# A linear-attention block gated by an MLP mixer: Gram products of the first two tiles beside WQ's column means, and w1's column means from rounded parts

## Chip, cores and metric

The kernel runs on one core of one Trainium2 chip. The metric is device time in microseconds (us) of one execution; lower is better. The kernel before was timed three times. One more execution was taken with the hardware profiler; its records are called the trace, and its summary the page.

## What is computed

The inputs are x (2048 rows of 512), the attention weights wqkv and wo, and the mixer weights w1 to w4. The core of the reference is this:

```python
xn = _layernorm(x)
# s: linear attention, 32 heads of width 16
q, k, v = heads(xn @ wqkv)
phi = lambda t: jnp.where(t > 0, t + 1, jnp.exp(t)) + 1e-6
kv = einsum("bhsd,bhse->bhde", phi(k), v)
z = einsum("bhsd->bhd", phi(k))
num = einsum("bhqd,bhde->bhqe", phi(q), kv)
den = einsum("bhqd,bhd->bhq", phi(q), z)[..., None] + 1e-6
s = (num / den) @ wo
# B: spatial-shift mixer, then channel MLP, both on xn
h = gelu(_layernorm(xn) @ w1)
x1 = xn + shift(h) @ w2        # quarters of h shifted by +1, -1, +2, -2 rows
B = x1 + gelu(_layernorm(x1) @ w3) @ w4
return x + s * silu(B)
```

## The kernel before

The 2048 rows are 16 tiles of 128 rows (`NT`), in four blocks of four tiles (`QT`). Nearly every product on TensorE is made from rounded parts: an fp32 operand is split into a high part of the type fp32r, copied by ScalarE (`pl.act(hi, ..., AF.Copy)`), and a low part, the rest, subtracted by VectorE (`split`). `rounded` does both. `products` then makes three products, high by high, high by low and low by high. A few products are made in plain fp32 (`slow=True`). In the trace one of these has two records.

The layer normalization is folded into the products. x is multiplied raw (transposed, as `xt`), and its column means enter through the weights: `Weights.center` adds up the four 128-row chunks of a weight (tile `wqt` for WQ, `w1t` for w1), multiplies the sum by a matrix of ones (PSUM tile `wqm` or `w1m`, line 577) and subtracts the mean from the chunks (line 579). For WQ the sum is made by three VectorE additions; for w1, with `by_dma`, by one load and three accumulating DMAs on GpSimd's queue. The K weights are treated another way: their column sums (`wkt`, then `ksum`) become the tile `wneg`, and `feature_k` subtracts the mean of each row times that sum.

The first part of the program, up to about 80 us, is written in this order. WK and the transposed x of block 0 are loaded (`load_u(0, 2)`, in two pieces) and split. `load_rows` loads the first four row tiles, and ScalarE forms their sums (`sq`, with the helper columns `sx`) and squared sums. `raw_k` and `project` make the keys k0 to k3. `feature_k` turns them into features (tiles `kt`, `kr`, and the parts k0h, k0l and so on), and `halves_x` splits the normalized rows (x0h, x0l). Then WQ is centered and split, `gram(i)` adds the products of x and k of tile i to the four PSUM accumulators g (12 products a tile), and `query(i)` makes the queries (12 products a tile). Blocks 1 to 3 follow; w1 is centered in block 1 after key 6. The mixer's second product (`mix2`), the first MLP product (`up_pair`) and the product of queries and attention matrix (`attend_pair`) are made in Strassen form by the function `seven`: PSUM banks pb, pa and pe (with the suffix m in `mix2`, s in `attend_pair`) are filled in turns and read out by ScalarE or VectorE between two uses (tiles p1, p5, u2).

The order of instructions on each engine isn't the order in which the program is written. All operations are first recorded by `Plan.add`, each with an estimated cost; `deadlines` gives each a due time, worked backwards from the order of the TensorE operations; `nudged` makes some of them due earlier or later, by the table `SOONER` (pairs of operation number and steps of 0.25 us); and `emit` plays through the schedule and writes the instructions out one by one. A TensorE operation may go ahead of older ones within limits (`window` us of nominal TensorE time, `ahead` for those that take a new buffer), and a loading operation may start `lead` us before it is due. A changed table or limit can therefore move any instruction of any engine. What each engine issues is fixed at build time, and each engine's queue runs in order: an instruction that waits holds up all behind it.

The lines which the change touches are 565 to 579 (`Weights.center`), 1223 to 1234 (WQ, the Gram products and the queries), and 1413 to 1423 (the table and the limits). L146 in the profile is the line on which every matmul is issued, L167 every ScalarE operation, L189 to L199 the VectorE ones, L205 to L223 the DMAs.

Of the kernel before, what the change touches and what calls it, by code (L numbers as in the profile page):

```python
# [393 lines left out]
def linear_attn_gated_by_mixer(  # L394
# [43 lines left out]
    pl = Plan(nc, pools, counts, ("acc", "mm"))  # L438

    def piece(name, dt=F32):  # L440
        return pl.new("p", name, dt, PIECE)[:, :512]

    def rounds(name):

        return piece(name + "h", F32R), piece(name + "l", F32R)
# [4 lines left out]
    def bank(name):  # L450
        return pl.new("mm", name, F32, 512)[:, :]

    def fixed(name, n, dt=F32):

        t = pl.new("const", name, dt, n)
        t.ap = const.tile([P, n], dt, name=name)
        return t

    def both(pair, a, z):

        return tuple(v.cols(a, z) for v in pair)
# [5 lines left out]
    def split(out, full, hi):  # L467
        pl.tt(out, full, hi.f32, ALU.subtract)

    def products(ps, terms, start=True, stop=True, more=False, behind=None):  # L470

        ms = []
        for sh, sl, mh, ml in terms:
            ms += [(sh, mh), (sh, ml), (sl, mh)]
        for n, (s, m) in enumerate(ms):
            pl.mm(ps, s, m, start and n == 0, stop and n == len(ms) - 1, more=more, behind=None if n else behind)

    def rounded(hi, lo, full, src=None):

        pl.act(hi, src or full, AF.Copy)  # L480
        split(lo, full, hi)
# [9 lines left out]
    ident, ones, nhalf, zacc = fixed("ident", P), fixed("ones", P), fixed("nhalf", QT), fixed("zacc", 512)  # L491
    identr = fixed("identr", P, F32R)
    onesr, bmask, tiny, zmore = fixed("onesr", P, F32R), fixed("bmask", P), fixed("tiny", 1), fixed("zmore", 1)
# [45 lines left out]
    class Weights:  # L539
# [25 lines left out]
        def center(self, by_dma=False):  # L565

            t, r = piece(self.name + "t"), self.raw
            if by_dma:
                pl.load(t, self.src[:, 0])
                for c in range(1, NC):  # L570
                    pl.gather(t, self.src[:, c])
            else:
                pl.tt(t, r[0], r[1], ALU.add)
                pl.tt(t, t, r[2], ALU.add)
                pl.tt(t, t, r[3], ALU.add)
            ps = bank(self.name + "m")
            pl.mm(ps, ones.all, t, True, True, slow=True)
            for c in range(NC):
                pl.stt(r[c], ps, -1.0 / D, r[c], ALU.mult, ALU.add)

# [15 lines left out]
    def scale_x(lo, n):  # L596

        r = rs1[:, lo:lo + n]
        w = small(f"w{lo}", n).all
        pl.ts(w, var(mv1, lo, lo + n), EPS, None, ALU.add, eng="POOL")  # L600
        power(r, w, n)
        pl.ts(ns1[:, lo:lo + n], r, -1.0, None, ALU.mult, eng="POOL")
        pl.tt(nm1[:, lo:lo + n], means(mv1, lo, lo + n), ns1[:, lo:lo + n], ALU.mult, eng="POOL")
        for i in range(lo, lo + n):
            halves_x(i)
# [59 lines left out]
    def project(ps, i, ws, cs):  # L665
        b, j = divmod(i, QT)
        a = 2 + j * P
        products(ps, [ut(b, c, a, a + P) + ws.chunk(c) for c in cs], 0 in cs, NC - 1 in cs)
# [69 lines left out]
    def feature_k(i, ps):  # L738

        t, r = piece(f"kt{i}"), piece(f"kr{i}")  # L740
        pl.stt(t, wneg.all, mean(mv1, i), ps, ALU.mult, ALU.add)
        pl.act(r, t, AF.Relu, scale=col(rs1, i))
        pl.act(t, t, AF.Exp, scale=col(rs1, i))
        hi, lo = rounds(f"k{i}")
        pl.stt(r, t, 1.0, r, ALU.min, ALU.add)
        pl.act(hi, r, AF.Identity, bias=tiny.all)
        pl.stt(lo, r, TINY, hi.f32, ALU.add, ALU.subtract)
        pl.gather(zacc.all, r)
        GK[i] += (hi, lo)
# [14 lines left out]
    def query(i):  # L764
        ps = bank(f"q{i}")
        project(ps, i, WQ, range(NC))
        e, r = piece(f"qe{i}"), piece(f"qr{i}")
        pl.act(by_block(e), by_chunk(ps), AF.Relu, scale=col(ns1, i))
        pl.act(by_block(r), by_chunk(ps), AF.Relu, scale=col(rs1, i))
        pl.act(e, e, AF.Exp, scale=-1.0)  # L770
        pl.soon(pl.store(pqd[i].all, r))
        pl.soon(pl.gather(pqd[i].all, e))

    def gram(i):
        xh, xl, kh, kl = GK.pop(i)
        for c in range(NC):
            products(G[c].all, [both((xh, xl), c * P, (c + 1) * P) + (kh, kl)], i == 0, i == NT - 1)
# [442 lines left out]
    for i in range(2, QT):  # L1220
        project(ks[i], i, WK, range(1, NC))
        feature_k(i, ks[i])
    WQ = Weights("wq", wqkv[0])
    WQ.center()
    WQ.split()
    gram(0)
    query(0)
    query(1)
    load_u(1, 1)
    load_rows(QT)  # L1230
    scale_x(QT, 1)
    gram(1)
    query(2)
    gram(2)
    query(3)
# [69 lines left out]
    for base, s in ((0, 1), (DH - 1, -1)):  # L1305
        v = bmask.all.via(lambda ap: ap.rearrange("p (h d) -> p h d", d=DH))
# [16 lines left out]
    for gg in range(NC):  # L1323
        cs = gg * P, (gg + 1) * P
        ps = bank(f"kv{gg}").cols(0, P)
# [4 lines left out]
    for gg in range(NC):  # L1330
        ps = bank(f"m{gg}")
# [10 lines left out]
    for b in range(NQ):  # L1342
# [50 lines left out]
        else:  # L1393
# [3 lines left out]
            t = piece(f"xi{i}", F32R)  # L1397
# [13 lines left out]
                gate(b * QT + QT - 1, a, o, D // 2, late=True, by_dma=False, whole=o > 0)  # L1411

    SOONER = (
# [7 lines left out]
    )  # L1421
    pl.emit(first=6.0, lead={"p": 12.0, "w": 10.0, "ab": 10.0}, reserve={"p": 8, "w": 1, "ab": 0}, window=7.0,
            ahead=3.0, table=SOONER)


# [35 lines left out]
```

## Time and profile before

| | |
|---|---|
| time, median of 3 runs | 523.48 us (523.04 to 523.54) |
| time of the profiled execution | 523.29 us |
| its span, first to last instruction | 521.5 us |
| VectorE busy | 375.0 us (72%) |
| ScalarE busy | 328.7 us (63%) |
| GpSimd busy | 112.2 us (22%) |
| DMA | 100.11 MB, mean 192 GB/s |

The span starts with the program's first instruction; the profiled execution's time is 1.8 us longer than it. PE is TensorE's matmuls, PEld its weight loads, DVE is VectorE, ACT ScalarE, POOL GpSimd and SP SyncE. Rows of the timeline give start, length, engine, line, operation, written tile <- read tiles, and in brackets the idle time ahead and who ended it. Buffer numbers are left out of names: `k` can be k0 to k15, `w_s` a raw chunk of w1 or w2. The matmul records overlap, since matmuls are pipelined: the time that one takes from TensorE is read from start to start.

### The profile page before, as it was taken

The page shows a single profiled execution, that of the slowest core. Times are in us where ns is not written, and L with a number is a line of the kernel's source. Part 1 is how long each engine was busy: PE and PEld are TensorE (multiplying, and loading weights), DVE is VectorE, ACT ScalarE, POOL GpSimd, SP SyncE. Part 2 cuts the span into 40 slices and gives each one's busy share as a digit, 9 for nine tenths or more (in the row PEclk, how much of TensorE's full clock was granted, in tenths as well). Part 3 has the DMA queues.
Part 4 walks back from the last instruction along what each step waited for, and adds up shares of the span by engine and source line. Part 5 has one row for each costly group of instructions (what it writes and reads, how often), then busy time and mean ns, then how long its engine had stood idle before and what let it go on. Part 6 is the DMA issues. An engine that isn't in the chain of part 4 may idle for free.

```text
span 521.5 us, 8876 instructions
## 1 busy us (share of the span) xinstructions
PE 514.3 (99%) x3011; PEld 445.8 (85%) x3011; DVE 375.0 (72%) x748; ACT 328.7 (63%) x669; POOL 112.2 (22%) x207
## 2 busy tenths in 40 slices
PE   8999999999999999999999999999999999999996
PEld 5777788988888888898999889899898898999985
DVE  4974697559475837899998458886567867496635
ACT  5899784769558837769865656466463456544621
POOL 1777253140272022211100022000040000310000
PEclk9999999999999999999999999999999999999999
DMA  7959993375887189999685969848489466898704
GB/s 239 291 126 200 225 234 81 79 165 186 184 197 168 34 192 240 268 242 264 232 265 183 264 161 202 266 134 203 119 172 313 147 182 129 200 288 251 230 1 121
DMA packets 73856, 100.11 MB, mean 192 GB/s; under 512 B 7908, under 2 KB 31988, under 8 KB 73812
## 3 DMA queue, kind: packets, MB, share of 16 engines
q1 hardware_dynamic: 62724, 79.37, 49.5%
q0 software_dynamic: 11088, 20.19, 23.4%
q8 instruction: 23, 0.38, 0.3%
q14 instruction: 21, 0.17, 0.1%
HBM read 60.33 MB, written 30.81 MB: 175 GB/s over the span
## 4 chain that ended last, share of the span: by engine, by line
PE 93%; ACT 3%; DMA 2%; SPq 1%; DVE 1%; issue 1%; DVEq 0%; ACTq 0%
PE acc L146 23%; PE pb L146 11%; PE h L146 9%; PE g L146 8%; PE q L146 8%; PE pe L146 6%; PE k L146 5%; PE pbm L146 4%; PE pbs L146 3%; PE pa L146 3%; PE pem L146 2%; PE s L146 2%; PE a L146 2%; PE pes L146 2%; DMA wk_s<-in_wqkv 1%; PE pam L146 1%
## 5 line engine op out<-in xcount | busy, mean ns | idle before, releaser
L223 POOL DMA_DIRECT2D xo<-x1d x12 | 10.7, 1179 | 166.6 <-ACT xo L167 166.6
L223 POOL DMA_DIRECT2D th<-in_x x14 | 12.1, 868 | 72.2 <-DVE th L199 51.4
L167 ACT ACTIVATE p<-pb 128x256 f32<-128x256 f32 x20 | 7.7, 383 | 31.5 <-PE pb L146 31.4
L223 POOL DMA_DIRECT2D zacc<-kr x16 | 15.4, 963 | 52.4 <-DVE kr L199 43.5
L223 POOL DMA_DIRECT2D o<-x x16 | 14.6, 930 | 41.8 <-ACT o L167 19.9
L167 ACT ACTIVATE gf<-gf 128x256 f32<-128x256 f32 (+1 forms) x40 | 20.9, 523 | 0.9
L199 DVE SCALAR_TENSOR_TENSOR kt<-wneg,mv,k 128x512 f32<-128x512 f32 x16 | 11.8, 745 | 11.2 <-PE k L146 11.1
L167 ACT ACTIVATE ht<-ht 128x512 f32<-128x512 f32 x16 | 10.0, 630 | 15.5 <-DVE ht L189 15.5
L223 POOL DMA_DIRECT2D pqd<-qe x16 | 15.0, 938 | 19.6 <-DMA pqd<-qr 5.2
L199 DVE SCALAR_TENSOR_TENSOR kr<-kt,kr 128x512 f32<-128x512 f32 x16 | 11.1, 691 | 10.7 <-ACT kt L167 10.6
L167 ACT ACTIVATE th<-xo 128x512 f32<-128x512 f32 (+1 forms) x16 | 9.8, 616 | 13.4 <-DVE xo L189 11.7
L167 ACT ACTIVATE p<-pe 128x256 f32<-128x256 f32 x20 | 7.7, 384 | 12.3 <-PE pe L146 12.3
L189 DVE TENSOR_TENSOR gf<-pa,p 128x256 f32<-128x256 f32 x20 | 8.4, 422 | 9.3 <-ACT p L167 4.8
L189 DVE TENSOR_TENSOR ht<-h,abc 128x512 f32<-128x512 f32 x16 | 10.7, 687 | 5.8 <-PE h L146 5.3
L167 ACT ACTIVATE qe<-q,ns 128x512 f32<-128x512 f32 x16 | 10.9, 681 | 5.5 <-PE q L146 5.5
L167 ACT ACTIVATE x<-x,nm,rs 128x512 f32<-128x512 f32 x16 | 12.3, 807 | 3.2 <-POOL nm L189 3.2
L167 ACT ACTIVATE kr<-kt,rs 128x512 f32<-128x512 f32 x16 | 11.5, 717 | 3.6 <-DVE kt L199 3.5
L588 DVE BATCH_NORM_STATS2 st<-o 128x6 f32<-128x512 f32 x16 | 10.8, 686 | 3.2 <-DMA o<-x 3.2
L189 DVE TENSOR_TENSOR gf<-u,pe 128x256 f32<-128x256 f32 x20 | 8.3, 416 | 6.3 <-PE pe L146 6.3
L199 DVE SCALAR_TENSOR_TENSOR th<-th,so 128x512 f32<-128x512 f32 (+1 forms) x17 | 11.1, 658 | 2.3 <-ACT th L167 1.4
L167 ACT ACTIVATE y<-o,nm,rs 128x512 f32<-128x512 f32 x16 | 12.2, 802 | 0.0
L167 ACT ACTIVATE kt<-kt,rs 128x512 f32<-128x512 f32 x16 | 11.6, 724 | 0.4
(1567 smaller groups left out, 2195.0 us busy)
## 6 DMA issues: line engine op xcount, KB each, us to landing
w_s<-in_w SPq DMA_DIRECT2D x28, 256.0 KB, 4.4
x<-in_x SPq DMA_DIRECT2D x16, 256.0 KB, 5.1
zacc<-kr POOLq DMA_DIRECT2D x16, 256.0 KB, 5.3
pqd<-qr SPq DMA_DIRECT2D x16, 256.0 KB, 3.2
pqd<-qe POOLq DMA_DIRECT2D x16, 256.0 KB, 5.4
o<-x POOLq DMA_DIRECT2D x16, 256.0 KB, 4.8
x1d<-o SPq DMA_DIRECT2D x16, 256.0 KB, 4.0
pq<-pqd SPq DMA_DIRECT2D x16, 256.0 KB, 4.4
```

The lines of the kernel that those rows point to most:

```text
L146: lambda: nc.tensor.matmul(out.get(), lhs.get(), rhs.get(), start=start, stop=stop, skip_group_check=more))
L167: nc.scalar.activation(out.get(), src.get(), func, scale=get(scale), **kw)
L189: self.vec(eng, out, [a, b], lambda: self.e(eng).tensor_tensor(out.get(), a.get(), b.get(), op=op), True)
L199: lambda: self.nc.vector.scalar_tensor_tensor(out.get(), a.get(), get(s), b.get(), op0=op0, op1=op1),
L223: lambda: self.nc.gpsimd.dma_start(out.get(), get(src), accum_op=ALU.add), mb=mb)
L588: pl.add("DVE", .62, .69, [xv], [st], lambda: nc.vector.bn_stats(st.get(), xv.get()))
```

## The change

There are three edits. In `center`, when the sum came by DMA (which is w1 alone), the sum is split into rounded parts first, and two fp32r products with `onesr` (ones in fp32r) take the place of one fp32 product. `gram(0)` is written ahead of `WQ.center()`, and `gram(1)` directly behind `WQ.split()` instead of behind `scale_x(QT, 1)`. The planner's table is replaced, and its limits: lead of the tags p and w from 12 and 10 to 10 and 20, window from 7 to 9, ahead from 3 to 6.

```diff
@@ -574,7 +574,13 @@
             ps = bank(self.name + "m")
-            pl.mm(ps, ones.all, t, True, True, slow=True)
+            if by_dma:
+                ts = rounds(self.name + "m")
+                rounded(*ts, t)
+                for n, v in enumerate(ts):
+                    pl.mm(ps, onesr.all, v, n == 0, n == 1)
+            else:
+                pl.mm(ps, ones.all, t, True, True, slow=True)
             for c in range(NC):
                 pl.stt(r[c], ps, -1.0 / D, r[c], ALU.mult, ALU.add)
@@ -1221,15 +1227,15 @@
     WQ = Weights("wq", wqkv[0])
+    gram(0)
     WQ.center()
     WQ.split()
-    gram(0)
+    gram(1)
     query(0)
     query(1)
     load_u(1, 1)
     load_rows(QT)
     scale_x(QT, 1)
-    gram(1)
     query(2)
     gram(2)
@@ -1411,16 +1417,15 @@
     SOONER = (
-        15, 3112, 16, 652, 20, 3160, 24, 308, 25, 137, 27, 308, 28, 136, 31, 160, 33, 309, 34, 277, 36, 43,
+        15, 4865, 16, 1223, 20, 4844, 24, 462, 25, 213, 27, 466, 28, 198, 31, 318, 33, 493, 34, 350, 36, 61,
...
     )
-    pl.emit(first=6.0, lead={"p": 12.0, "w": 10.0, "ab": 10.0}, reserve={"p": 8, "w": 1, "ab": 0}, window=7.0,
-            ahead=3.0, table=SOONER)
+    pl.emit(first=6.0, lead={"p": 10.0, "w": 20.0, "ab": 10.0}, reserve={"p": 8, "w": 1, "ab": 0}, window=9.0,
+            ahead=6.0, table=SOONER)
```

In the order that the planner writes out, these instructions move:

- TensorE: `wqm` stays where it was, directly behind the last key product and ahead of the Gram products of tile 0. The 12 Gram products of tile 1 move from between and behind the products of queries 0 and 1 to behind the first six products of query 0. `w1m` stays behind key 6, as two products. After that the order is the old one but for some dozens of products near the edges of `seven` blocks, which change places with products around them.
- SyncE's queue: at the start the pieces of WK go one place ahead of the pieces of `xt`, and the load of x0 moves from between wk_s2 and wk_s3 to behind xt0_3. The load of x7 moves ahead of those of block 1's `xt`, and that of x4 between them; the fourth query store goes ahead of w1's loads. Loads and stores from 60 us on change places by one or a few.
- ScalarE: the first row sums of tile 0 move behind wk_3h and u_3h; x1, k1h, x1h and the two squared sums of tiles 2 and 3 move ahead of wq_2h; u_0h of block 1 and the normalizations of x5 to x7 move back; the new rounding of `w1t` stands behind the second `ar` copy and ahead of kr5.
- VectorE: kr1, k1l and x1l move ahead of WQ's chunks 2 and 3; the new subtraction of `w1t` stands behind k4l and ahead of kt5.
- GpSimd's queue: some halo pieces change places with the first accumulating DMA of `zacc` and with those of `w1t`; the fourth query's DMA moves ahead of block 1's halo.

11 rows, old and new, of the table SOONER are left out of this document.

## Prediction

> **What bounds the kernel now.** I read the page first, then TensorE's waits, then the start-to-start times of its products at the places that the change touches.
>
> ```profile
> span 521.5 us, 8876 instructions
> PE 514.3 (99%) x3011; PEld 445.8 (85%) x3011; DVE 375.0 (72%) x748; ACT 328.7 (63%) x669; POOL 112.2 (22%) x207
> PEclk9999999999999999999999999999999999999999
> ```
> ```profile
> PE k L146 <- ACT u_3h L167: 0.4, 1, 0.4
> PE wqm L146 <- DVE wqt L189: 0.3, 1, 0.3
> PE k L146 <- DVE wk_1l L189: 0.2, 1, 0.2
> PE k L146 <- DVE wk_2l L189: 0.2, 1, 0.2
> PE k L146 <- ACT wk_2h L167: 0.2, 1, 0.2
> ```
>
> The reader is to see that TensorE sets the time: it is busy for 99% of the span at full clock, and its only idle stretches behind the warm-up are these five, 1.3 us in all, every one before the first Gram product. So the change can gain in two ways alone, by less work on TensorE or by less waiting, and most of the waiting lies in the first 20 us. It can lose in any place where a producer comes late for TensorE.
>
> **w1's column means.** The first three rows are the old product and its neighbours, the last three the nearest relatives of the new one: products with `onesr` of a sum in rounded parts, made for z.
>
> ```profile
> 60.53 1.02 PE L146 MATMUL w1m<-w1t,ones 128*128 128x512 f32 x2
> 60.98 0.80 PE L146 MATMUL q<-wq_0h,u_0h 128*128 128x512 f32 x1
> 61.62 0.40 PE L146 MATMUL q<-wq_0l,u_0h 128*128 128x512 f32 x1
> ...
> 221.07 0.39 PE L146 MATMUL zp<-zsh,onesr 128*128 128x512 f32 x1
> 221.30 0.40 PE L146 MATMUL zp<-zsl,onesr 128*128 128x512 f32 x1
> 221.53 0.29 PE L146 MATMUL pbm<-w_b11h,ha113h 128*128 128x256 f32 x1
> ```
>
> From 60.53 to 61.62 TensorE makes the fp32 product and one fp32r product of 512 columns: 1.09 us. An fp32r product takes 0.23 us (221.07 to 221.30). After the change that stretch holds three of them, 0.69 us. The gain is 1.09 - 0.69 = 0.40 us, and it is on the path, since TensorE doesn't idle there. [...]
>
> The new work, one ScalarE rounding and one VectorE subtraction of 128x512, must be hidden. In the new order the rounding stands behind the second `ar` copy and the subtraction behind k4l:
>
> ```profile
> L223 POOL DMA_DIRECT2D w1t<-in_w x3: 895/912/1224, 22.7 to 39.3; - x3
> DMA to landing us min/median/max: 5.0/5.7/5.8
> ```
> ```profile
> 51.40 0.62 ACT L167 ACTIVATE qe<-qe 128x512 f32<-128x512 f32 x1
> 53.16 0.72 ACT L167 ACTIVATE kr<-kt,rs 128x512 f32<-128x512 f32 x1 [1.14 <-DVE kt L199]
> ```
> ```profile
> 51.53 0.69 DVE L199 SCALAR_TENSOR_TENSOR k4l<-kr,k4h 128x512 fp32r<-128x512 f32 x1 [1.28 <-ACT k4h L167]
> 52.38 0.75 DVE L199 SCALAR_TENSOR_TENSOR kt<-wneg,mv,k 128x512 f32<-128x512 f32 x1 [0.16 <-PE k L146]
> ```
>
> The third accumulating DMA is issued at 39.3 and lands by 45.1, some 6 us before the rounding's turn. ScalarE then idles 1.14 us and VectorE 1.28 us, so 0.62 and 0.69 us fit; kt5, queued behind the subtraction, may start some 0.5 us later. w1m is due at 60.5, 8 us on. I cost this at nothing. If the cover were gone, all of tile 5's features would come 0.5 us later, and with them a Gram product several microseconds away.
>
> **The start.** The wqm product isn't moved: the planner takes what is ready, and in the new order the Gram products of tile 0 still come behind it. So the 0.3 us at wqm goes only if wqt comes sooner. These rows show what it hangs on:
>
> ```profile
> 12.93 0.62 ACT L167 ACTIVATE sq<-x 128x512 f32<-128x512 f32 x1
> ...
> 14.60 0.72 ACT L167 ACTIVATE sq<-x,sx 128x512 f32<-128x512 f32 x1 [0.66 <-DVE sx L194]
> ...
> 15.66 0.60 ACT L167 ACTIVATE wneg<-ksum 128x512 f32<-128x512 f32 x1
> ```
> ```profile
> 13.73 0.70 DVE L189 TENSOR_TENSOR wkt<-wkt,wk_s 128x512 f32<-128x512 f32 x1
> 14.35 0.14 DVE L194 TENSOR_SCALAR sx<-sx 128x1 f32<-128x1 f32 x1
> ...
> 19.28 0.69 DVE L189 TENSOR_TENSOR wqt<-wqt,wq_s 128x512 f32<-128x512 f32 x1
> ```
>
> ScalarE is the pace here: it waits 0.66 us for sx of tile 1, which VectorE makes only behind the last wkt addition, and then come the squared sum, a piece of u, and wneg, on which kt0, kr0 and the last wqt addition follow. With WK's pieces and xt0_3 loaded ahead of x0, the chunks 1 to 3 of K, and with them VectorE's splits and wkt, come earlier; tile 0's sums come later, as x0 now lands behind two more pieces. If the wkt work is out of the way by then, ScalarE's 0.66 us of idling vanish and wqm, with all behind it, comes 0.66 us sooner. If instead the sums of tile 0 now wait for VectorE as those of tile 1 do today, the idling is only moved: nothing. If x0's lateness adds to that idling, I bound the loss by half of the piece now idle, 0.3 us. I take 0.35 us of gain, the middle between none and all. TensorE's own waits for K (1.0 us in the four rows above) don't count besides: it would only reach wqm sooner and wait there.
>
> **Queries 0 and 1.** In the old order these products were just in time:
>
> ```profile
> 25.21 0.40 PE L146 MATMUL q<-wq_2h,u_2h 128*128 128x512 f32 x1
> ...
> 28.04 0.73 PE L146 MATMUL q<-wq_3h,u_3h 128*128 128x512 f32 x2
> 28.65 0.73 PE L146 MATMUL g<-k1h,x1h 128*128 128x512 f32 x2
> 29.22 0.39 PE L146 MATMUL q<-wq_3l,u_3h 128*128 128x512 f32 x1
> ```
> ```profile
> 23.32 0.62 ACT L167 ACTIVATE wq_2h<-wq_s 128x512 fp32r<-128x512 f32 x1
> 23.84 0.80 ACT L167 ACTIVATE x<-x,nm,rs 128x512 f32<-128x512 f32 x1
> ...
> 27.37 0.62 ACT L167 ACTIVATE wq_3h<-wq_s 128x512 fp32r<-128x512 f32 x1
> 27.89 0.71 ACT L167 ACTIVATE k1h<-kr,tiny 128x512 fp32r<-128x512 f32 x1
> ```
>
> The first pair takes 0.61 us and the second 0.57 where two products need 0.46: 0.15 and 0.11 us lost to wq_3h (ready at 27.99) and k1h (28.60). In the new order twelve Gram products, 12 x 0.23 = 2.8 us, stand where wq_2h was wanted, so wq_2h is needed 15 products or 3.45 us later; it had 25.21 - 23.94 = 1.27 us to spare. On ScalarE it falls behind x1 (0.80), k1h (0.71), x1h (0.62, as the copy of wq_2h) and two squared sums (0.72 each by the row at 14.60): 3.57 us. That leaves 1.27 + 3.45 - 3.57 = 1.15 us, less what ScalarE waits for sx of tile 2, now behind x1l on VectorE. So both losses of together 0.26 us go, and a new one of between none and 0.3 us can come at wq_2h; I take 0.15 us of gain.
>
> **The rest.** The exchanged loads, stores and fillers move no TensorE work in or out. At `seven`'s hand-overs of a PSUM bank they decide over tenths:
>
> ```profile
> 486.83 0.28 PE L146 MATMUL pbs<-m_t2h,q12s0l 128*128 128x256 f32 x1
> 487.11 0.39 PE L146 MATMUL pes<-m_b22h,q12s1h 128*128 128x256 f32 x1
> 487.33 0.28 PE L146 MATMUL pes<-m_b22l,q12s1h 128*128 128x256 f32 x1
> ```
> ```profile
> L167 ACT ACTIVATE p<-pe x20: 363/386/387, 243.9 to 491.8; 128x256 f32<-128x256 f32 x20
> ```
> ```profile
> L167 ACT ACTIVATE p5m<-pem x8: 362/372/386, 94.5 to 232.6; 128x256 f32<-128x256 f32 x8
> ```
> ```profile
> L167 ACT ACTIVATE p5s<-pes x6: 384/386/387, 351.0 to 497.5; 128x256 f32<-128x256 f32 x6
> ```
>
> The two products from 486.83 take 0.50 us to the start of the third, where 256 columns need 0.12 each (221.53 is such a product; half of 0.23): 0.26 us lost, because the read-out p5 was late. There are 20 + 8 + 6 = 34 such blocks. Both tables leave these read-outs early in ScalarE's queue mostly; I see no reason for a sign and take zero, with bounds of four blocks better (1.0 us) and nine blocks worse (2.3 us).
>
> **The sum.** 0.40 + 0.35 + 0.15 = 0.90 us off the profiled execution's 523.29 us: 522.4 us. That execution lies 0.19 us under the median of 523.48, within the spread of the three runs. The bounds of the terms together: w1m 0.40 in any case, the start from +0.66 to -0.3, the queries from +0.26 to -0.1, the rest from +1.0 to -2.3.
>
> **Rivals.**
>
> 1. Only w1m counts, 522.9 us: ScalarE's idling at the start is only moved to another wait, and what the queries gain at wq_3h they pay at wq_2h. For it: the chain through sums, wneg and kt0 has the same instructions as before, and wqm keeps its place, so this edit doesn't do what its wording says. Against it: VectorE's wkt work gets its operands earlier.
> 2. The hand-overs improve too, 521.4 us: four blocks of the kind at 486.83 no longer wait, 4 x 0.26 = 1.0 us. For it: the wider window lets more filling products go ahead. Against it: the waits view counts no idling there, and most blocks lose less than this one.
> 3. Slower, 524.7 us: ScalarE or VectorE stands in another operation of 0.6 to 0.8 us when a bank is to be read out, in nine blocks more than before, 9 x 0.26 = 2.3 us on top of the 522.4. It decides from 1.08 + 1.05 = 2.1 us or eight blocks. For it: in the new order rounds of w3 or of y stand ahead of p5 and u2 at several blocks where they stood behind. Against it: fillers stand between the last product of a bank and its next use.
>
> **How the numbers follow.** About 0.2%, or 1.05 us, is what a measurement of this kernel can tell from no change: faster begins under 522.43, slower over 524.53. The forecast has a chance of 0.48; it sits at that edge, and since its terms can only be sized from neighbours, I count 0.33 of it as faster and 0.15 as within. Rival 1 has 0.15, within; rival 2 0.15, faster; rival 3 0.22, of which 0.20 slower. Faster is 0.33 + 0.15 = 0.48, within 0.15 + 0.15 + 0.02 = 0.32, slower 0.20. The forecast's own range is 521.8 to 523.0. To leave out no more than 2 in 10 the range takes in rivals 2 and 3 with 0.4 us below the first and 0.1 above the second: 521.0 to 524.8.
>
> **What would show it.** In the changed kernel's trace, from the first w1m product to the second product of query 6 three steps of 0.23 us; no idle stretch of TensorE for w1ml. wqm should start at about 19.75 instead of 20.11, with ScalarE's idle 0.66 us gone; if wqm starts at 20.1, the start's term was wrong. Behind wqm the Gram products of tile 1 should run without a wait, and the step at wq_2h should lose less than 0.15 us. Between 62 and 512 us the same products should take the same time within 0.5 us; if they take 1.5 us more with the steps at pe's and pb's second use over 0.2 us, rival 3 holds. The forecast is wrong, whatever the total, where the start loses or the stretch behind 62 us gains more than the two edits together.

## The result, and the profile after

| | before | changed |
|---|---|---|
| median, 21 runs each on one chip | 523.62 us (522.81 to 524.24) | 524.55 us (523.98 to 527.28) |
| ratio | | 1.0022 [1.0015, 1.0029] |
| profiled execution | 523.29 us | 527.28 us |
| its span | 521.5 us | 525.4 us |

The change made the kernel slower, by 0.93 us or 0.22%, and the interval of the ratio lies clear of 1. The profiled execution is the longest of the 21: what it shows is the kind of loss, not the usual size of it. The page of the changed kernel, as quoted of before:

```profile
span 525.4 us, 8878 instructions
PE 516.0 (98%) x3011; PEld 446.8 (85%) x3011; DVE 375.7 (72%) x749; ACT 328.5 (63%) x670; POOL 118.6 (23%) x207
PEclk9999999999999999999899999999999999999999
```

TensorE has as many records as before (the fp32 product for w1 had two, the two that replace it have one each) and is still the bound, but the clock has an 8 in one slice of 13 us, just at the middle. TensorE's waits (us in total, times, longest) have another look:

```profile
PE pb L146 <- ACT p L167: 1.0, 1, 1.0
PE pbm L146 <- ACT p1m L167: 0.9, 1, 0.9
PE k L146 <- DVE u_1l L189: 0.7, 1, 0.7
PE pe L146 <- ACT p L167: 0.5, 1, 0.5
PE k L146 <- ACT u_2h L167: 0.2, 1, 0.2
PE pem L146 <- ACT p5m L167: 0.2, 1, 0.2
```

Before, all five waits lay ahead of the first Gram product. Now wqm has none, and three of 0.5 to 1.0 us stand where a PSUM bank of a `seven` block is read out by ScalarE. The two edits that were sized do what they should. wqm starts at 19.58 us where it started at 20.11, and w1m has three steps of 0.23 and 0.24 us:

```profile
19.58 1.10 PE L146 MATMUL wqm<-wqt,ones 128*128 128x512 f32 x2
...
60.10 0.40 PE L146 MATMUL w1m<-w1mh,onesr 128*128 128x512 f32 x1
60.34 0.39 PE L146 MATMUL w1m<-w1ml,onesr 128*128 128x512 f32 x1
60.57 0.39 PE L146 MATMUL q<-wq_0h,u_0h 128*128 128x512 f32 x1
60.80 0.39 PE L146 MATMUL q<-wq_0l,u_0h 128*128 128x512 f32 x1
```

Where the time went is seen from the lag: the start of a product in the changed kernel less the start of the same product before, in us, by the start of before. Such a table is worked out from two traces, and later experiments are read the same way (e13 is the changed kernel, profiled once more):

| product, start before | changed | e13 | e5 | e6 | e10 | e11 |
|---|---|---|---|---|---|---|
| Gram of tile 4, 55.7 | -0.42 | -0.66 | -0.70 | +0.25 | -0.87 | -0.99 |
| Gram of tile 5, 65.8 | -0.83 | -1.08 | -1.12 | +0.25 | -1.28 | -1.41 |
| pam0, 92.9 | -0.72 | -0.96 | -1.01 | +0.26 | -1.17 | -1.30 |
| query 8, 98.5 | +0.39 | +0.15 | -1.04 | +1.17 | -0.06 | -1.25 |
| pam12, 222.8 | -0.20 | -0.34 | -1.13 | +1.11 | -0.60 | -1.86 |
| pb0_1, 252.8 | +0.07 | -0.09 | -1.13 | +1.12 | -0.33 | -1.60 |
| acc0_2, 264.6 | +3.40 | +1.75 | -1.14 | +1.08 | -0.16 | -1.42 |
| accx, 516.7 | +3.89 | +2.17 | -1.19 | +0.89 | +0.12 | -1.21 |

The changed kernel is ahead by 0.83 us at 66 us, loses 1.1 us between 93 and 98, and 3.3 us between 253 and 265. The early rows of kernels with the same start differ by up to 0.6 us, so a column is read by its steps.

**The loss at 93 us** begins on ScalarE at 81. Its rows, first of before, then of the changed kernel:

```profile
77.26 0.63 ACT L167 ACTIVATE u_3h<-xt 128x512 fp32r<-128x512 f32 x1
77.91 1.28 ACT L167 ACT_TABLE_LOAD   x1
81.89 0.63 ACT L167 ACTIVATE ht<-ht 128x512 f32<-128x512 f32 x1 [2.70 <-DVE ht L189]
```
```profile
81.17 1.28 ACT L167 ACT_TABLE_LOAD   x1 [3.06 <-DVE ht L189]
82.46 0.63 ACT L167 ACTIVATE ht<-ht 128x512 f32<-128x512 f32 x1
```

The first GELU (`ht0_0`, in place) has a table load of 1.28 us ahead of it on ScalarE. Before, that load ran from 77.91 to 79.19, while ScalarE was waiting anyway. Now it starts only when VectorE has made ht (81.17), and the GELU stands behind it. VectorE was 0.72 us sooner (81.17 to 81.89), yet the GELU is 0.57 us later. The reason is in the built programs, where each instruction stands with its waits:

```
before    LoadActFuncSet                 ht_0<-ht_0 [waits DVE]
changed   LoadActFuncSet [waits DVE]     ht_0<-ht_0 [waits Activation]
```

In the changed order the planner's buffer for `ht0_0` is number 37, which xt2_2 had before it and ScalarE had read (u2_2h). The built program has two waits here, one for ScalarE on the GELU and the one for VectorE on the load ahead of it. Before, the buffer was number 76 (x6l), which ScalarE hadn't touched, and the one wait was on the GELU. In both programs the load stands directly ahead of the GELU; only the wait has moved. That the buffer is the cause is tested by e5 and e6.

**The loss at 253 us** begins on GpSimd at 249, with `nm` for the last four row tiles (128x4 elements). First before, then changed:

```profile
247.67 1.69 POOL L594 TENSOR_TENSOR rs<-w,nhalf 128x4 f32<-128x4 f32 x1
249.44 0.28 POOL L189 TENSOR_TENSOR nm<-mv,rs 128x4 f32<-128x4 f32 x1
```
```profile
247.62 1.34 POOL L600 TENSOR_TENSOR rs<-w,nhalf 128x4 f32<-128x4 f32 x1
249.04 3.09 POOL L189 TENSOR_TENSOR nm<-mv,rs 128x4 f32<-128x4 f32 x1
252.22 0.23 POOL L194 TENSOR_SCALAR nm<-nm 128x4 f32<-128x4 f32 x1
```

Meanwhile VectorE (changed kernel) has one operation behind the other, until den:

```profile
249.51 0.68 DVE L189 TENSOR_TENSOR w_al<-w_s,w_ah 128x512 fp32r<-128x512 f32 x1
250.11 0.68 DVE L189 TENSOR_TENSOR w_s0l<-w_sf,w_s0h 128x512 fp32r<-128x512 f32 x1
250.72 0.41 DVE L189 TENSOR_TENSOR w_sf<-w_s,w_s 128x256 f32<-128x256 f32 x1
251.05 0.42 DVE L189 TENSOR_TENSOR w_sf<-w_s,w_sf 128x256 f32<-128x256 f32 x1
251.39 0.68 DVE L199 SCALAR_TENSOR_TENSOR qz<-pq,zb 128x512 f32<-128x512 f32 x1
252.10 0.69 DVE L1088 TENSOR_REDUCE den<-qz 128x32 f32<-128x512 f32 x1
```

An operation that takes 0.28 us before takes 3.09 here and ends as den begins. ScalarE's y, which need nm, are late with it, and so is p, the read-out that TensorE waits for:

```profile
252.49 1.52 ACT L167 ACTIVATE y<-o,nm,rs 128x512 f32<-128x512 f32 x2 [1.55 <-POOL nm L194]
253.92 0.61 ACT L167 ACTIVATE w_s1h<-w_sf 128x512 fp32r<-128x512 f32 x1
254.44 0.80 ACT L167 ACTIVATE y<-o,nm,rs 128x512 f32<-128x512 f32 x1
255.14 0.36 ACT L167 ACTIVATE p<-pb 128x256 f32<-128x256 f32 x1
```

Before, p ran nearly two microseconds sooner:

```profile
253.29 0.36 ACT L167 ACTIVATE p<-pb 128x256 f32<-128x256 f32 x1
```

The rest of the 3.3 us is the clock. The windows of the changed kernel's profile, with PEclk in the third column from the end, and of e13, the same kernel again:

```profile
core 0: us, PE busy (x) PEld busy (x) DVE busy (x) ACT busy (x) POOL busy (x), PEclk, DMA share, GB/s
256.00:258.00 2.00, 1.48 (x11) 1.27 (x10) 2.00 (x5) 2.00 (x7) 0.00 (x0) 0.91 0.00 0
258.00:262.00 4.00, 4.00 (x25) 4.00 (x24) 3.15 (x7) 0.66 (x3) 0.00 (x0) 0.62 0.64 243
```
```profile
256.00:258.00 2.00, 1.48 (x13) 1.27 (x12) 2.00 (x5) 2.00 (x6) 0.00 (x0) 1.00 0.00 0
258.00:262.00 4.00, 4.00 (x36) 4.00 (x36) 3.93 (x9) 2.05 (x5) 0.00 (x0) 1.00 0.81 305
```

With the same idle time ahead, TensorE starts 25 products in the four microseconds of the first and 36 in those of the second. By an estimate, (1 - 0.62) x 4 us, that is some 1.5 us of work lost, and 3.40 - 0.07 = 3.3 us of loss in the first profile stands against 1.75 + 0.09 = 1.8 in e13. The single microseconds from 258 to 261 us read 0.50 in the first, and e13 has 1.00 over the whole stretch, so waits of one and the same length were followed by the drop once and once not. The waits of 1.0 and 0.5 us were followed by no fall in the profiles of e3 (mean clock of the run 0.999) and e7 (1.00 from 258 to 262 us) too, and by the fall in that of e1 (0.65). What decides it, no run shows.

### The profile page after: what moved, and what is told of

Read it like the earlier page. It is cut to its first block, busy times and chain, and to the rows that moved or that the text cites. A ratio compares the mean times of both kernels' runs of the same rounds, so it can differ in the third digit from the quotient of the medians.

```text
span 525.4 us, 8878 instructions
## 1 busy us (share of the span) xinstructions
PE 516.0 (98%) x3011; PEld 446.8 (85%) x3011; DVE 375.7 (72%) x749; ACT 328.5 (63%) x670; POOL 118.6 (23%) x207
## 4 chain that ended last, share of the span: by engine, by line
PE 89%; ACT 4%; DMA 2%; DVE 2%; issue 1%; SPq 1%; DVEq 0%; ACTq 0%
PE acc L146 22%; PE pb L146 11%; PE q L146 9%; PE g L146 7%; PE h L146 7%; PE k L146 7%; PE pe L146 5%; PE pbm L146 4%; PE pbs L146 3%; PE pa L146 3%; PE a L146 2%; PE pem L146 2%; PE s L146 2%; PE pes L146 1%; DMA wk_s<-in_wqkv 1%
## 5 line engine op out<-in xcount | busy, mean ns | idle before, releaser
L167 ACT ACTIVATE gf<-gf 128x512 f32<-128x512 f32 (+1 forms) x40 | 20.8, 522 | 0.8
L223 POOL DMA_DIRECT2D pqd<-qe x16 | 16.1, 1028 | 17.2 <-ACT kr L167 5.8
L189 DVE TENSOR_TENSOR f_10l<-gf,f_10h 96x512 fp32r<-96x512 f32 x4 | 2.7, 686 | 23.7 <-PE pb L146 15.6
L167 ACT ACTIVATE xo<-acc 128x512 f32<-128x512 f32 x12 | 7.2, 598 | 9.9 <-PE acc L146 9.0
```

Source lines behind the costliest of these rows:

```text
L167: nc.scalar.activation(out.get(), src.get(), func, scale=get(scale), **kw)
L189: self.vec(eng, out, [a, b], lambda: self.e(eng).tensor_tensor(out.get(), a.get(), b.get(), op=op), True)
L223: lambda: self.nc.gpsimd.dma_start(out.get(), get(src), accum_op=ALU.add), mb=mb)
```

## Experiments

The planner would answer any edit with a new order. So each kernel has the order in which operations are written out as a list of numbers, taken from the planner's own order of the kernel before or of the changed one, and then one thing moved. Buffers are still handed out as before, so that some buffers further on change places.

```diff
-            best = None
...
-            s, op = best
+            op = ops[order[len(done)]]
```

Times are medians, beside the runs of the kernel before on the same chip:

| run | what it is | us | before | ratio |
|---|---|---|---|---|
| e1 | the changed kernel again | 526.16 | 523.20 | 1.0051 [1.0038, 1.0064] |
| e2 | changed order to 76 us, old order behind | 522.85 | 523.20 | 0.9991 [0.9983, 1.0000] |
| e3 | old order to 76 us, changed order behind | 524.62 | 523.20 | 1.0028 [1.0016, 1.0039] |
| e4 | old order, w1m alone changed | 523.08 | 523.20 | 0.9993 [0.9985, 1.0002] |
| e5 | e2, table load early | 522.13 | 523.53 | 0.9974 [0.9966, 0.9983] |
| e6 | before, table load late | 524.17 | 523.53 | 1.0012 [1.0003, 1.0021] |
| e7 | changed, qz four operations sooner | 525.41 | 523.53 | 1.0036 [1.0024, 1.0049] |
| e8 | changed, p10_1 sooner | 527.71 | 523.53 | 1.0082 [1.0068, 1.0096] |
| e9 | changed, qz five operations sooner | 525.31 | 523.30 | 1.0043 [1.0030, 1.0055] |
| e10 | changed, nm on VectorE | 523.67 | 523.30 | 1.0006 [0.9997, 1.0015] |
| e11 | e10, table load early | 522.28 | 523.30 | 0.9983 [0.9975, 0.9992] |
| e12 | changed to 222 us, load early, old order behind | 522.67 | 523.26 | 0.9991 [0.9982, 1.0000] |
| e13 | the changed kernel once more | 525.69 | 523.26 | one run |

**e1 to e4: which part of the order.** e1 has no edit. e2 and e3 exchange the order behind tile 7's last Gram product. e4 has the order of before with the new rounding and the two products put into it.

> The changed kernel once more, for a second profile. Theory (order): the new order loses behind 76 us, at ScalarE's read-outs of PSUM banks near 92 us and near 254 us; TensorE is again some 0.8 us ahead at 76 us and behind at 300 us, time about 0.9 us over the kernel before. Rival (chance): the 1.8 us lost at 254 us and the half-speed clock behind it belong to that one execution; then this profile has no such wait at 254 us and the loss has to be found elsewhere.

> The changed program in the changed order up to the last Gram product of tile 7 (about 76 us), and from there on in the order of the kernel before. Theory (order): the gain of the first 76 us stays, 0.8 us under the kernel before, 522.8 us. Rival (the new start isn't a gain that lasts): what is gained up to 76 us is lost in the next wait that was just in time, no more than 0.2 us under the kernel before.

> The changed program with the order of the kernel before up to the last Gram product of tile 7, w1's rounded sum included, and from there on the changed order. Theory (order): gain of 0.4 us from w1's product, loss of 1.7 us from the rest: 1.3 us over the kernel before, 524.9 us. Rival (the rest of the order is harmless): 0.4 us under it.

> The order of the kernel before throughout, with nothing but w1's column means from rounded parts (rounding behind the second ar copy, subtraction behind k4l, two products in place of one). Both theories: 0.4 us under the kernel before, if the two added conversions are hidden; no change, if a wait near 92 us takes it back.

e1 has the waits of the first profile, so they are no accident of one execution. On this chip the same kernel is 0.51% slower, not 0.22%, 3.0 us where 0.9 were expected. Its profile has the clock at 0.65 from 258 to 262 us. How often that happens can be read from the mean clock of each run: 0.995 or 0.996 in the two profiles with the fall, 0.997 or more in every run of the kernel before beside e1 to e13. By that mark the clock fell in 1 of the first 21 runs of the changed kernel, in 2 of e1's 6, 2 of e3's 11 and 4 of e8's 5. So the usual run has no fall, and the fall isn't what sets e1's time: its other four runs took 525.38 to 526.23 us. Why the loss is larger on this chip than on the first stays open.

e2 meets its 522.8 by luck, since the kernel before is faster on this chip: it is 0.35 us under it, not 0.8, and its trace sides with the rival. It leads by 1.11 us at pam0 and by 0.20 at query 8: the loss at 93 us comes with the changed start, since the buffer of `ht0_0` follows from it. e3 has no loss at 93 us (-0.25 before and behind it) but loses 1.9 us at 253 (-0.70 to +1.17): that loss comes with the changed rest, and 1.42 us over before is what its theory had. e3's profile is of its median run, with nm at 3.09 us and the clock full. e4's median is 0.12 us under before, less than the 0.40 by which its lag changes from 55.7 to 65.8 us (+0.17 to -0.23); it can't be told from no change. (Its profile is of its slowest run and also loses 1.1 us near 390 us, where ScalarE waits 1.12 and 1.03 us for loads of xo instead of 0.62 and 0.44.)

**e5 and e6: the table load.** `ht0_0` gets another free buffer, and nothing is moved. In e5 TensorE had read it last, in e6 ScalarE.

```diff
-                        t.slot = slots[tag].pop(0)[1]
+                        k = 2 if t.name == "ht0_0" else 0
+                        t.slot = slots[tag].pop(k)[1]
```

(In e6, k = 5.)

> The order of e2 (changed order up to tile 7's last Gram product, then the order of before); only ht0_0, the first tile that goes through the GELU, lies in another buffer, one whose last reader was TensorE (68 for 37), so that the GELU waits for VectorE alone. Theory (the ACT_TABLE_LOAD of 1.28 us stands behind a wait for VectorE when the GELU has to wait for two engines, and runs in idle time when it waits for one): the table load starts near 77.5 us, ht0_0's GELU near 80.8 instead of 82.09, p1m0 and p5m0 of the first mixer block follow up to a microsecond sooner, TensorE keeps its lead of 0.7 to 1.1 us past 98 us, and the time is 0.5 to 0.8 us under e2's: 522.1 to 522.4, about 1.0 under the kernel before. Rival (the row of ScalarE's and VectorE's work behind the GELU sets that stage, wherever the load lies): the load moves, but p1m0 stays at 92.8 within 0.2 us, and the time is e2's, 522.85 within 0.3.

> The kernel before in its own order; only ht0_0 lies in another buffer, the one of xt2_2, which ScalarE read last (36 for 76), so that the GELU waits for VectorE and for ScalarE's own earlier read. Theory: the table load of 1.28 us moves from 77.9 us to behind VectorE's ht0_0 (near 81.9), the GELU starts near 83.2 instead of 81.89, p1m0 follows 0.7 to 1.3 us late, TensorE is as much late at 98 us and to the end: 524.2 to 524.9. Rival: the chain has slack or the load stays where it was: 523.6 within 0.3. The buffers of some 120 later tiles change places too, which both hold for nothing.

ScalarE in e5, then in e6:

```profile
77.84 1.28 ACT L167 ACT_TABLE_LOAD   x1
80.84 0.63 ACT L167 ACTIVATE ht<-ht 128x512 f32<-128x512 f32 x1 [1.72 <-DVE ht L189]
```
```profile
82.16 1.28 ACT L167 ACT_TABLE_LOAD   x1 [4.57 <-DVE ht L189]
83.45 0.63 ACT L167 ACTIVATE ht<-ht 128x512 f32<-128x512 f32 x1
```

And the read-out p1m at the end of that row of work, in the kernel before and in e6 (the numbers behind the colon are its length in ns, then its start):

```profile
L167 ACT ACTIVATE p1m<-pbm x1: 386/386/386, 93.0 to 93.0; 128x256 f32<-128x256 f32 x1
```
```profile
L167 ACT ACTIVATE p1m<-pbm x1: 363/363/363, 94.1 to 94.1; 128x256 f32<-128x256 f32 x1
```

Both came as the theory had it. In e6 p1m comes 1.1 us later, 0.9 of it from the load's place, since e6 was 0.25 late from the start, and TensorE goes from +0.26 to +1.17; the time is 0.64 us over before, the lag at the end less the 0.25 of the start. Its 524.17 lies just under the lower end of what was expected. In e5 the lead of 1.0 us goes through to the end, and the kernel beats both: 0.26% under before. The row behind the GELU, the rival's bound, simply starts sooner. The new buffer makes some 120 later tiles change places too; behind 98 us both lags stay within 0.35 us of their value there to the end, so that costs little.

**e7 to e9: what makes nm long, and who holds TensorE.** e7 puts qz ahead of four operations, directly behind f_10l as in the kernel before; e9 one operation sooner still, ahead of f_10l; e8 leaves VectorE alone and moves a read-out on ScalarE. VectorE's order in e7:

```diff
 f0_10l
+qz2
 w3_1_al
 w3_1_s0l
 w3_1_sf1
 w3_1_sf1
-qz2
 den2
```

ScalarE's in e8:

```diff
+p10_1
 y13
 y12
 w3_1_s1h
 y14
-p10_1
```

> The changed kernel in its own order; only VectorE's qz of the second query tile (one operand in PSUM) stands four operations sooner, ahead of the four with all operands in SBUF, as in the kernel before. Theory (GpSimd's nm of 128x4 takes 3.09 us because VectorE runs one operation with two SBUF inputs behind the other, and gets through beside or behind qz): nm takes under 1.3 us, y13 and y12 start near 250.9 instead of 252.49, p10_1 near 253.6 instead of 255.14, TensorE's waits there (1.16 and 0.69 us) shrink by 1.2 us or more and the clock does not fall behind them: 1.2 to 2.5 us less than the changed kernel, 522.4 to 523.4. Rival (nm is long for another cause, or ScalarE's order alone makes p10_1 late): nm stays at 3 us or p10_1 stays within 0.3 us of 255.14, and the time is the changed kernel's, 524.5 or more. The loss near 92 us stays in either case.

> The changed kernel in its own order; only the read-out p10_1 of a PSUM bank stands sooner on ScalarE, ahead of the two normalizations y13 and y12 that wait for nm, and of w3_1_s1h and y14. Theory (TensorE is held by the read-out that stands behind the waiting normalizations): nm still takes 3.09 us and y13 still starts near 252.5, but p10_1 runs in ScalarE's idle time before it, TensorE's wait of 1.16 us at the bank goes, and p50_1's of 0.69 us at least by half: 1.2 to 2.5 us less than the changed kernel, 522.5 to 523.6. Rival (the normalizations themselves, or VectorE behind them, are what is late): TensorE waits as long in another place within 3 us, and the time is the changed kernel's within 0.4.

> The changed kernel in its own order; only VectorE's qz of the second query tile stands one operation sooner than in e7, ahead of f_10l, so that it runs when nm comes up on GpSimd (248.9 to 249.6 us in the changed kernel's profile, nm at 249.04). Theory, narrowed by e7, where nm was already waiting when qz came and stayed shut out (3.08 us): nm gets through only if it comes up while VectorE is in an operation that does not have two SBUF inputs, as in the kernel before; it takes under 0.8 us here, y13 starts near 250.9, p10_1 near 253.6, and TensorE's two waits (1.0 and 0.5 us) go: 522.7 to 523.6. Rival (qz lets nothing through, and nm was short in the kernel before for another cause): nm stays at 2 to 3 us and the time at 524.5 or more. f_10l comes 0.6 us later, which may cost TensorE up to 0.1 us.

All three missed; e7 and e9 came out as their rivals had it, with nm at 3 us and over 524.5 us. In e7 nm (3.08 us from 248.69) lasted through the whole of qz (249.16 to 249.84). In e9 it even started while qz ran, and took as long; GpSimd and VectorE there:

```profile
248.52 3.09 POOL L189 TENSOR_TENSOR nm<-mv,rs 128x4 f32<-128x4 f32 x1
```
```profile
248.39 0.68 DVE L199 SCALAR_TENSOR_TENSOR qz<-pq,zb 128x512 f32<-128x512 f32 x1
248.99 0.68 DVE L189 TENSOR_TENSOR f_10l<-gf,f_10h 96x512 fp32r<-96x512 f32 x1
...
251.47 0.68 DVE L1057 TENSOR_REDUCE den<-qz 128x32 f32<-128x512 f32 x1
```

In the changed kernel, e3, e7 and e9 nm ends within 0.14 us of den's start (252.13 and 252.10 in the changed kernel), wherever qz stands; in e8, with VectorE's order unchanged, it was done after 2.15 us, 0.9 us ahead of den. The expectation of e7 gives qz an operand in PSUM, and that of e9 builds on it. By the kernel's text it has none: pq and zb come from the pool p, which isn't one of the two in PSUM, and pq is filled by a DMA (issued at 240.75 us before, 242.09 in the changed kernel). So neither run tests whether it matters where an operation's inputs lie; they show that qz's place alone doesn't make nm short. In the kernel before, nm (249.44 to 249.72) ran beside qz (248.98 to 249.66) and on into w_al (from 249.58). That VectorE's row shuts nm out was the author's reading of these times; why nm takes 3.09 us beside one row and 0.28 beside the other is not shown.

e8 tells about TensorE. nm was done sooner here, but p10_1, now first in ScalarE's queue, waited for its own product until 252.88, and the y stood behind it:

```profile
PE pe L146 <- ACT p L167: 2.5, 1, 2.5
```

One wait of 2.5 us took the place of 1.0 and 0.5: the second read-out, p50_1, stands behind the y as well, and they had become later. So it isn't p10_1's place that holds TensorE; all of ScalarE's row behind nm is late.

**e10 and e11: nm off GpSimd.** The two operations of nm for the last four tiles go to VectorE, behind f_10l.

```diff
+        on = "DVE" if b == 3 else "POOL"
-        pl.tt(m, means(mv2, a, z), r, ALU.mult, eng="POOL")
-        pl.ts(m, m, -1.0, None, ALU.mult, eng="POOL")
+        pl.tt(m, means(mv2, a, z), r, ALU.mult, eng=on)
+        pl.ts(m, m, -1.0, None, ALU.mult, eng=on)
```

e11 has e5's line too (k = 2).

> The changed kernel in its own order; only the two small operations of nm for the last four tiles (128x4) run on VectorE, behind f_10l, and not on GpSimd. Theory (nm on GpSimd is late because VectorE's row shuts it out, and everything behind it on ScalarE is late with it): nm is done by 250.2 us, y13 starts near 250.9 instead of 252.49, p10_1 near 253.6 instead of 255.14, TensorE's waits of 1.0 and 0.5 us go, the clock does not fall: the lead over the kernel before at 260 us is 0.1 to 0.4 us instead of a lag of 1.5 or more, and the time is 522.9 to 523.4. Rival (the order of ScalarE's row, w_s1h and y14 ahead of p10_1, holds TensorE without nm's help): the waits stay above 1 us in all, 524.3 or more. The table load of the GELU stays late in both, 1.0 to 1.1 us.

> e10 and, with it, ht0_0 in a buffer that TensorE read last (68 for 37, as in e5): the changed kernel in its own order with both suspected losses taken out. Theory (these two places are all that the changed order lost): the lead over the kernel before is about 1.1 us from 66 us to the end; 522.0 to 522.5, as e5. Rival (the changed order loses in a third place behind 262 us, near 357 or 367 us, where e7 and e8 lagged 0.4 us more): 522.6 to 523.2.

VectorE and ScalarE in e10:

```profile
249.11 0.15 DVE L189 TENSOR_TENSOR nm<-mv,rs 128x4 f32<-128x4 f32 x1
249.30 0.17 DVE L194 TENSOR_SCALAR nm<-nm 128x4 f32<-128x4 f32 x1
249.37 0.69 DVE L189 TENSOR_TENSOR w_al<-w_s,w_ah 128x512 fp32r<-128x512 f32 x1
```
```profile
250.45 1.51 ACT L167 ACTIVATE y<-o,nm,rs 128x512 f32<-128x512 f32 x2
251.87 0.62 ACT L167 ACTIVATE w_s1h<-w_sf 128x512 fp32r<-128x512 f32 x1
252.39 0.80 ACT L167 ACTIVATE y<-o,nm,rs 128x512 f32<-128x512 f32 x1
253.09 0.36 ACT L167 ACTIVATE p<-pb 128x256 f32<-128x256 f32 x1
```

The y start two microseconds sooner than in the changed kernel, p is ahead of where it was before, and TensorE's waits view has no row between 250 and 262 us. With the same order on ScalarE the loss at 253 us is gone (-0.33 to -0.16 in the table), which rules the rival out. The time is level with before, 0.3 us over what was expected. e11 takes the table load out as well and is 1.39 us faster than e10 on the same chip, 0.17% under before: the two places are what turned the gain into a loss. Its lead shrinks from 1.86 us at 222 us to 1.21 at the end in steps of 0.3 near 224 and some 0.4 near 353 us, so a little of the rival holds too.

**e12 and e13: what was left.**

> The changed program, emitted in the changed order up to the product pbm12 near 222 us, behind it in the order of before, and ht0_0 in the buffer that TensorE read last (68). e11, the changed order with both losses out, led the kernel before by 1.86 us at 222 us in its profile and by 1.21 at the end. Theory (the changed order is as good as that of before or better up to 222 us, and what it loses lies behind it, in nm near 249 us and in smaller steps near 228, 357 and 367 us): nm is short (0.3 us) on GpSimd without any further edit, the lead of 1.7 to 1.9 us at 222 us stays to the end within 0.3, and the time is 521.5 to 522.0. Rival (the old order behind 222 us gives the lead back, since it waits for loads or ScalarE's row there): 522.1 to 522.6, as e5.

> The changed kernel itself, one more look. Its runs stand at 523.98 to 526.00, most at 524.3 to 524.9, but its two profiled runs took 527.28 and 526.86. Theory A (nm is shut out for some 3 us in every run, and the runs differ in whether the clock falls behind it): nm near 3 us, time 525.0 to 525.5 without the fall and above 526 with it. Theory B (how long nm is shut out differs from run to run): a run under 525.0 with nm well under 3 us. A third long profile would leave the usual run unseen.

e12 missed: nm is short again (0.28 us), but at the seam from 222.8 to 228.7 us the lead falls from 1.50 to 0.84, and the time is within 0.1 us of the rival's range. e5 stays the best of the versions run. e13 took 525.69 us with nm at 3.09 us and full clock, as theory A had it, 0.2 us over its range. All three profiles of the changed kernel have the long nm, and none is of a run as short as the median of the first 21. By the medians, e10 against the changed kernel, the usual run lost 0.93 - 0.37 = 0.6 us there; whether nm is shorter in it was not seen.

## Why the prediction was wrong

The forecast was 522.4 us with "faster" as the likeliest sign; it came out 2.15 us higher, inside the range.

- **w1's column means: right.** 0.40 us was forecast; the lag changes by 0.41 between the Gram products of tiles 4 and 5, in the changed kernel as in e5 and e10, and by nothing in e6, which has the old product. The added rounding and subtraction were hidden.
- **The start: right in sign, mis-sized.** 0.35 us was forecast for wqm. It came 0.53 us sooner in the first profile and up to 1.12 (e11) in the others with the new start, more than the bound of 0.66. Only one stretch had been counted, ScalarE's 0.66 us ahead of tile 1's squared sum. That stretch didn't vanish, it moved to tile 0:

```profile
12.35 0.73 ACT L167 ACTIVATE sq<-x,sx 128x512 f32<-128x512 f32 x1 [0.63 <-DVE sx L194]
```

By the forecast's own words such a move was to bring nothing. The gain came from WK's pieces: wk_3h ran at 9.95 us instead of 11.21 (9.35 in e11), so that the row behind it, wneg at 15.15 instead of 15.66, was sooner all the same.
- **Queries 0 and 1: the wrong sign, by little.** 0.15 us of gain was forecast. From wqm to the products behind 31 us the lead shrinks by some 0.1 us in every kernel with the new start. The step at wq_2h loses 0.03 us, as forecast, but the two steps ahead of tile 1's first Gram product take 0.32 and 0.34 us (24.22 to 24.88), and x1h is ready only at 24.83. Start and queries together bring 0.9 us where 0.5 was forecast: at the Gram product of tile 4 the eleven profiles with the new start lead by 0.77 us in the mean (0.42 to 0.99), and the four with the old start, the kernel before among them, are 0.12 late.
- **The rest: the step that failed.** It said that the exchanged fillers, loads and stores "move no TensorE work in or out", saw "no reason for a sign" and took zero. It looked for small losses at 34 hand-overs. There were two large ones, at one block each: 1.1 us behind the table load and 1.8 us behind nm, 3.3 when the clock fell too (in the usual one of the first 21 runs, by the medians, some 0.6). They don't come from operations that stand in the way of a read-out, but from what ScalarE's row waits for: a wait that the buffer's last reader put ahead of a table load, and nm, which took 3.09 us on GpSimd beside VectorE's new row. The small steps that the forecast looked for are there in both directions, and for them the zero was right: in e11 0.4 us gained near 131 us at a block's hand-over, 0.3 lost near 224, 0.4 near 353, 0.3 gained near 495 and some smaller ones leave the lead of 1.25 at query 8 at 1.21. Without the two losses (e11) the change gains 1.02 us. That this is close to the 0.90 of the sum is partly luck: the start brought more than its term, and 0.16 us went between 66 and 98 us.
- **Rival 3** had the sign and, by chance, the size: 524.7 us. It was to be nine blocks of 0.26 us, with ScalarE busy in another operation. It was a ScalarE that stood idle, waiting for VectorE's ht and for GpSimd's nm, with the read-out queued behind.
- The first of the two losses could have been read ahead of time: the wait on the table load stands in the built program. The prediction went by which instructions move, not by what each waits for and which buffer it has.

## What to carry to other kernels

When a planner gives out buffers, compare the waits of two built programs as well as their order: a buffer's last reader can put a wait on an instruction that hasn't moved, and on a table load ahead of it (here the load went from 77.91 us to 81.17). Look for tiny operations on GpSimd that a long row of work depends on, and at how long they take in the new order; here 0.28 us became 3.09, and moving the two operations to VectorE cost 0.3 us there. A wait of the bounding engine can be followed by a loss beyond its length: behind 1.5 us of waits TensorE had a clock of 0.62 for 4 us in the first profile, another 1.5 us by the estimate above, and full clock in e13.

## What the runs showed of the hardware

- The 1.28 us of the table load ahead of `ht0_0`'s GELU fell into ScalarE's idle time where the buffer's last reader wasn't ScalarE (start at 77.91 before, 77.84 in e5). Where it was, the load started only behind VectorE's ht (81.17 changed, 82.16 in e6), and the GELU came behind it (82.46, 83.45).
- Waits of 1.0 and 0.5 us of TensorE were followed by a clock of 0.62 for 4 us in one profile and by full clock in another of the same kernel; in the first the fall to 0.50 lasted some 3 us.
- GpSimd's 128x4 multiplication for nm took 3.09 us in the changed kernel, e1, e3, e9 and e13, 3.08 in e7, 2.15 in e8 and 0.28 in the kernel before, e2, e4, e5 and e12. On VectorE it took 0.15 us (e10, e11).
